# Two large load buffers of a decode-attention kernel begin at multiples of 512 bytes in a partition

## Chip, cores, metric

The kernel runs on one core of one Trainium2 chip. The metric is the device time of one execution in microseconds (us), given as the median of several executions.

## The reference

The kernel computes one decode step of grouped-query attention (2 batches, 32 query heads, 8 key/value heads, 32768 cached positions, head size 128) and a small MLP on the same normalised input, and multiplies the two. Cut to what matters:

```python
def _A_ref(x, k_cache, v_cache, wq, wo):       # x (2,1,512), caches (2,8,32768,128), all bf16
    q = (x @ wq)                               # 32 heads of 128
    scores = einsum("bhqd,bhkd->bhqk", q, k) * Dh ** -0.5
    o = einsum("bhqk,bhkd->bhqd", softmax(scores), v)
    return o @ wo
...
return x + s * silu(mlp(xn))                   # s = _A_ref(xn, ...)
```

The two caches are 268 MB together, and every byte is used once. One query position per batch makes the arithmetic small, so the time to bring the caches in from HBM (the chip's main memory) is what counts.

## The kernel before

Of the sixteen (batch, head) groups, each has one 8 MB load of K and one of V. Every load puts 65536 contiguous bytes into each of the 128 partitions of SBUF, the memory that the compute engines work from. Sixteen DMA engines carry the loads. K lives in `kbuf`, V in `vbuf`; the weights are loaded into parts of the same two buffers that are free at the time. All sizes in `pers` are handed out one after the other in each partition, in the order of the program.

```python
    pers = ctx.enter_context(tc.tile_pool(name="pers", bufs=1))
    ...
    kbuf = pers.tile([128, 3 * SLOT], BF16, name="kbuf")      # SLOT = 16384 elements, 32768 bytes
    vbuf = pers.tile([128, 2 * SLOT], BF16, name="vbuf")
    Ts = [pers.tile([128, RT * NB * 32], I32, name=f"T{i}") for i in range(T_BUFS)]
    # ... some 40 smaller tiles follow

        def load_k(m):
            base = (m % 2) * SLOT
            src = row_view(A_k_cache, *groups[m])             # 128 x 65536 bytes, contiguous
            if m < last:
                d_k[m % 2].after(sp.dma_start(out=kbuf[:, base:base + 2 * SLOT], in_=src), 16)
            # ... the last group goes as two halves
        def load_v(m):
            ...
                sp.dma_start(out=vbuf[:, :], in_=src).then_inc(s_v, 16)
    ...
        for m in range(1, NG):                                # the SP queue issues all these loads
            wait(sp, (p_t, NT * (m - 1) + NR))                # half of K(m-1) has been used
            load_k(m)
            wait(sp, (p_o, m))                                # V(m-1) has been used
            load_v(m)
        # ... then the output projection's weights, wo, in 4096-byte pieces, into kbuf
```

The vector engine (DVE) transposes K in 32x32 blocks, the matrix engine (PE) makes scores, the scalar engine (ACT) takes the exponential, and PE multiplies with V.

The softmax here doesn't subtract the row's maximum and nothing guards it: scores larger than these inputs give would overflow.

## Time and profile before

| | before |
|---|---|
| median of 3 runs (first measurement) | 661.21 us (660.96 to 661.62) |
| span of the profiled run | 659.8 us |
| bytes read | 280.5 MB, mean 425 GB/s |
| PE, DVE, ACT busy | 60%, 51%, 8% |
| load queue's share of sixteen DMA engines | 98.5% |

These are lines of the page of the kernel before. The rows of digits cut the span into 40 equal slices and give the busy share of each in tenths (9 is 90% or more). PEclk is the granted clock of PE in tenths. The last line is a DMA queue: its packets, its megabytes, and the time that its packets took as a share of sixteen engines over the span.

```profile
span 659.8 us, 6521 instructions
...
PE 393.7 (60%) x2684; PEld 165.5 (25%) x2684; DVE 337.0 (51%) x428; ACT 50.3 (8%) x152; POOL 5.7 (1%) x18
...
PE   0538195683829558282865828376481947648765
...
DVE  2347191744809165380926539083562908447650
...
PEclk9999787785978769597885959779596976959795
DMA  8999999999999999999999999999999999999994
GB/s 366 434 443 441 434 445 421 421 445 433 441 442 405 441 434 441 441 445 401 441 433 445 441 413 429 438 441 441 441 401 445 433 445 437 417 429 430 421 421 197
...
q1 hardware_dynamic: 6408, 280.50, 98.5%
```

The DMA row is at 9 from the second slice to the last but one, and the queue's share is 98.5%. PE and DVE have nearly empty slices, and PE's clock falls to half in some, all without any dip of DMA that lasts. The kernel is limited by its loads.

This line of the table of waits has engine, tile and line, what it waited for, the total in us, how often, and the longest. DVE stood idle 150.5 us for K:

```profile
DVE T L449 <- DMA kbuf<-in_A_k_cache_dram: 150.5, 17, 11.4
```

The trace also records each DMA packet with its size and duration. The pages do not print the durations, so they are tabulated here. Here one packet is the bytes of one piece of contiguous destination in one partition (the texts below also call it a descriptor).

| bytes of a packet | packets | shortest | median | mean (ns) |
|---|---|---|---|---|
| 65536 (K and V) | 3840 | 2416 | 2421 | 2422.6 |
| 32768 (wq, last group) | 640 | 1211 | 1216 | 1233.1 |
| 14336 (MLP weights) | 256 | 535 | 535 | 535.1 |
| 4096 (wo) | 1024 | 159 | 161 | 163.3 |

The sum over all of them is 649.8 us for each of sixteen engines. The end of the span, in order of time (start, us, engine, line, operation; in brackets the idle time before it and what ended it):

```profile
...
645.00 3.59 PE L503 MATMUL bank<-vbuf,pt 128*16 128x512 bf16 x32 [5.08 <-DMA vbuf<-in_A_v_cache_dram]
...
652.50 3.58 PE L540 MATMUL bank<-kbuf,oX 128*2 128x128 bf16 x128 [0.47 <-DVE oX L473]
...
656.46 0.29 DVE L549 TENSOR_TENSOR out<-sg,x 98x128 bf16<-98x128 f32 x1
```

PE waits for the second half of the last V load, until 645.00. From there to the end of the arithmetic at 656.75 it is a chain of small steps, 11.75 us long.

### The profile page before, as it was taken

Reading aid. Unit: us, or ns where it says so; the run is one execution under the profiler, and the core shown is the slowest. Engines: PE = TensorE matmul, PEld = TensorE weight load, DVE = VectorE, ACT = ScalarE, POOL = GpSimd, SP = SyncE. Lnnn points to the kernel's source line nnn. Section 1 sums busy time; section 2 is a strip of 40 time slices with the busy share of each in tenths; the row PEclk is TensorE's granted clock in tenths of the full one; section 3 lists DMA queues with packets and bytes.
Section 4 is the critical chain, followed back from the end, with each engine's and each line's share of the span. In section 5 each row is a group of like instructions: output and inputs, shape, how many; then the busy total and the mean of one; then the engine's idle time right before and its main releaser. Section 6 shows DMA issues by size and latency. Waiting matters only on the chain. (4 is left out here: it accounts for less than half of the span.)

```text
span 659.8 us, 6521 instructions
## 1 busy us (share of the span) xinstructions
PE 393.7 (60%) x2684; PEld 165.5 (25%) x2684; DVE 337.0 (51%) x428; ACT 50.3 (8%) x152; POOL 5.7 (1%) x18
## 2 busy tenths in 40 slices
PE   0538195683829558282865828376481947648765
PEld 0513132231313223031322303132131322213223
DVE  2347191744809165380926539083562908447650
ACT  0111001010100101010010101001010010101000
POOL 1200000000000000000000000000000000000000
PEclk9999787785978769597885959779596976959795
DMA  8999999999999999999999999999999999999994
GB/s 366 434 443 441 434 445 421 421 445 433 441 442 405 441 434 441 441 445 401 441 433 445 441 413 429 438 441 441 441 401 445 433 445 437 417 429 430 421 421 197
DMA packets 6443, 280.64 MB, mean 425 GB/s; under 512 B 664, under 2 KB 672, under 8 KB 1696
## 3 DMA queue, kind: packets, MB, share of 16 engines
q1 hardware_dynamic: 6408, 280.50, 98.5%
q8 instruction: 5, 0.08, 0.1%
q14 instruction: 6, 0.05, 0.0%
q10 hardware_dynamic: 24, 0.01, 0.0%
HBM read 280.50 MB, written 0.00 MB: 425 GB/s over the span
## 5 line engine op out<-in xcount | busy, mean ns | idle before, releaser
L486 PE MATMUL bank<-T,z 128*128 128x512 bf16 x1024 | 283.1, 428 | 184.7 <-PEq L45 179.6
L449 DVE STREAM_TRANSPOSE T<-kbuf 128x1024 int32<-128x1024 int32 x256 | 290.6, 1206 | 150.5 <-DMA kbuf<-in_A_k_cache_dram 150.5
L486 PEld LDWEIGHTS bank<-T,z 128*128 128x128 bf16 x1024 | 99.3, 104 | 362.0 <-issue 283.6
L503 PE MATMUL bank<-vbuf,pt 128*16 128x512 bf16 x1024 | 68.2, 426 | 5.1 <-DMA vbuf<-in_A_v_cache_dram 5.1
L466 DVE RECIPROCAL rec<-bank 128x4 f32<-128x4 f32 x16 | 2.9, 182 | 114.2 <-PE bank L513 114.2
L423 ACT ACTIVATE ep<-bank 128x512 bf16<-128x512 f32 x32 | 19.1, 598 | 482.2 <-PE bank L486 482.2
L503 PEld LDWEIGHTS bank<-vbuf,pt 128*16 128x16 bf16 x1024 | 26.4, 98 | 38.8 <-issue 12.6
L457 DVE STREAM_TRANSPOSE pt<-ep 128x512 bf16<-128x512 bf16 x32 | 22.1, 691 | 20.2 <-ACT ep L423 20.2
L496 PE MATMUL bank<-sm,ones_f 128*128 128x4 f32 x64 | 9.4, 252 | 27.6 <-PEq L45 27.6
L513 PE MATMUL bank<-sel_o,ob 128*128 128x4 f32 x128 | 17.2, 258 | 12.5 <-PEq L45 12.5
L513 PEld LDWEIGHTS bank<-sel_o,ob 128*128 128x128 f32 x128 | 16.3, 199 | 20.5 <-issue 20.5
L496 PEld LDWEIGHTS bank<-sm,ones_f 128*128 128x128 f32 x64 | 8.5, 192 | 35.4 <-issue 35.4
L431 ACT COPY ob<-bank 128x512 f32<-128x512 f32 x16 | 9.4, 586 | 87.6 <-PE bank L503 87.6
L411 ACT COPY z<-qr 32x16 bf16<-32x16 bf16 x64 | 12.6, 197 | 0.6
L286 PE MATMUL bank<-ident,xn_bf 2*128 2x2 bf16 x4 | 0.3, 166 | 16.7 <-POOL x L277 16.7
L519 PE MATMUL bank<-on,sel_r 128*128 128x4 bf16 x64 | 3.9, 164 | 9.0 <-PEq L45 9.0
L423 ACT ACTIVATION_READ_ACCUMULATOR ep<-bank 128x1 f32 x32 | 6.3, 198 | 0.2
L470 DVE TENSOR_TENSOR xm<-bank,mask 128x16 f32<-128x16 f32 x16 | 2.8, 175 | 6.8 <-PE bank L519 6.8
L245 DVE CAST xf<-x_bf 128x512 f32<-128x512 bf16 x1 | 0.4, 427 | 11.4 <-DMA x_bf<-in_A_x_dram 11.4
L462 DVE TENSOR_SCALAR sm<-sel_h,rs 128x4 f32<-128x4 f32 x32 | 6.0, 188 | 0.0
L519 PEld LDWEIGHTS bank<-on,sel_r 128*128 128x128 bf16 x64 | 2.9, 97 | 9.9 <-issue 9.9
L322 PE MATMUL bank<-xT,kbuf 128*128 128x2 bf16 x128 | 3.6, 165 | 2.0 <-DVE xT L316 2.0
(64 smaller groups left out, 50.2 us busy)
## 6 DMA issues: line engine op xcount, KB each, us to landing
kbuf<-in_A_k_cache_dram SPq DMA_DIRECT2D x2, 4096.0 KB, 23.7
vbuf<-in_A_v_cache_dram SPq DMA_DIRECT2D x2, 4096.0 KB, 28.9
kbuf<-in_A_wq_dram SPq DMA_DIRECT2D x1, 4096.0 KB, 12.2
vbuf<-in_B_w_dram SPq DMA_DIRECT2D x2, 1792.0 KB, 17.9
kbuf<-in_A_wo_dram SPq DMA_DIRECT2D x1, 2048.0 KB, 38.3
kbuf<-in_A_wo_dram SPq DMA_DIRECT2D x1, 1536.0 KB, 41.5
kbuf<-in_A_wo_dram SPq DMA_DIRECT2D x1, 512.0 KB, 42.1
kbuf<-in_A_k_cache_dram SPq DMA_DIRECT2D x15, 27.7
```

Of the source, the lines that this page charges most:

```text
L322: i = pe.matmul(qT_ps[:, h * B:(h + 1) * B], lhsT=wq3[:, k, h * Dh:(h + 1) * Dh], rhs=xT[:, k, :], start=(k == 0), stop=(k == DK - 1),)
L411: i = act.copy(out=z[32 * j:32 * j + 32, :, :, c:c + rep], in_=qr[32 * j:32 * j + 32, :, :, b, g * rep:(g + 1) * rep],)
L423: act.activation(out=eps_[i][:, :], in_=sc[i][:, :], func=ACT.Exp, scale=inv_sqrt_dh, accum_out=rss[NPART * (m % 2) + i][:, :],)
L431: act.copy(out=ob[:, :], in_=o[:, :]).then_inc(s_ob, 1)
L449: dve.transpose(out=Ts[n % T_BUFS][:, :].rearrange("p (b t k) -> p t b k", b=NB, t=RT), in_=kt[:, r * W:(r + 1) * W].rearrange("p (t b k) ...
L457: dve.transpose(out=pts[h][:, :, :].rearrange("p r (t h) -> p t r h", h=rep), in_=eps_[i][:, :].rearrange("p (t r h) -> p t r h", r=NR, h= ...
L462: dve.tensor_scalar_mul(out=sms[h][:, :], in0=sel_h[:, :], scalar1=rss[NPART * (m % 2) + i][:, 0:1]).then_inc(s_p, 1)
L486: last_mm = pe.matmul(sc[i][:, :], lhsT=z[:, nb, e, zc:zc + 128], rhs=Tb[:, nb, :, e], start=(r == 0 and nb == 0 and e == 0), stop=(r == N ...
L496: pe.matmul(S, lhsT=ones_f[:, :], rhs=sms[h][:, :], start=(h == 0), stop=(h == NPART - 1))
L503: last_mm = pe.matmul(o[32 * j:32 * j + VT * rep, :], lhsT=pts[h][:, r, a * VT * rep:(a + 1) * VT * rep], rhs=vt[:, u * VT:(u + 1) * VT, : ...
L513: last_mm = pe.matmul(oT, lhsT=ob[:, t * Dh:(t + 1) * Dh], rhs=sel_o[:, t, :], start=(t == 0), stop=(t == VT - 1))
L519: last_mm = pe.matmul(xp[:, r, :], lhsT=sel_r[:, r, :, :].rearrange("p j w -> p (j w)"), rhs=on[:, :], start=True, stop=True,)
```

## The change

The intent: begin the destinations of the large loads on a round address, in case the DMA engines write faster there.

```diff
+PAD = 384
 ...
     psum = ctx.enter_context(tc.tile_pool(name="psum", bufs=1, space=bass.MemoryType.PSUM))
 
+    pers.tile([128, PAD // 4], F32, name="pad")
     kbuf = pers.tile([128, 3 * SLOT], BF16, name="kbuf")
     vbuf = pers.tile([128, 2 * SLOT], BF16, name="vbuf")
```

In the built programs, K moves from byte 16512 of a partition to 16896 and V from 114816 to 115200. Before, both are 128 past a multiple of 512 and also 128 past a multiple of 256. Every later tile moves by the same 384 bytes. Instructions, waits, DMAs and packets stay as they were.

## The prediction

> **What bounds the kernel now.** The DMA engines, from end to end. The profile's queue table gives the load queue 98.5% of sixteen engines' span; the 40-slice table shows DMA at 9 in all slices but the first and last, with 401 to 446 GB/s in the slices between. The compute engines have slack: PE 60%, DVE 51%, ACT 8% busy. The table of waits agrees: DVE idles 150.5 us for K loads. The granted clock falls to 0.5 in slices, which costs nothing here, as PE is not the limit.
>
> The trace's records of DMA packets say the same more sharply. The load queue has 3840 packets of 65536 bytes (mean 2423 ns), 640 of 32768 (1233 ns), 1024 of 4096 (163 ns) and 256 of 14336 (535 ns). Their durations sum to 649.8 us per engine, in a span of 659.8. Idle engine time inside the stream is under 1 us. What is left, about 10 us, is the start before the first packet (some 2 us) and the tail after the last (the output projection, 3.6 us of matmuls; two vector operations; the store).
>
> **What the change does.** Built both ways, K moves from byte 16512 of a partition to 16896, V from 114816 to 115200: from 128 past a multiple of 512 (also 128 past a multiple of 256) to a multiple of 512. Everything allocated later moves by 384 bytes too. The order of instructions on every engine, the waits, the number of DMAs, their bytes and packets are the same. So only the duration of one packet can change.
>
> **How much is there to win.** Medians, 65536 bytes against 4096: 2421 - 161 = 2260 ns for 61440 bytes, 27.19 bytes/ns, or 435 GB/s over 16 engines. The Trainium skill, "DMA: Bandwidth & Descriptors", "Where 436 GB/s comes from", puts the ceiling of the ports at 435.2; the trace agrees, so the bytes of a packet already move at that ceiling in spite of the misaligned start. Off that slope there is an intercept of about 10 ns a packet. If alignment costs anything it hides in these 10 ns. The same page, "How a descriptor splits into AXI transactions", says a descriptor that starts off a 256-byte boundary pays a partial first transaction and a leftover, once per descriptor and not once per 256 bytes. An estimate from its 32-byte beats: 4 extra beats on 2048, 0.2%, about 5 ns of 2421; no run yet shows that this holds for the write side in SBUF.
>
> There are 5760 packets, 360 per engine. At 5 ns each that is 1.8 us; all of the 10 ns is 3.6 us (0.5%). All of it would be on the critical path, since DMA is. More likely the intercept is a fixed cost of a packet, and the gain is near zero. Shifts of the other tiles touch DVE, PE and ACT only, whose time is hidden.
>
> **Predicted time:** 660.4 us, 8 in 10 between 657.2 and 662.4. Faster by over 2%: 1%. Within 2%: 98%. Slower by over 2%: 1%.
>
> **What the profile will show.** If right: the mean of 65536-byte packets stays between 2411 and 2425 ns, the load queue's share stays at 98 to 99%, the average at 424 to 427 GB/s, the transpose of K stays at 1202 ns, the waits keep their sizes. If alignment pays its estimated beats: 65536-byte packets about 5 ns shorter, and 4096-byte packets by the same 5 ns rather than in proportion. Wrong, if 65536-byte packets fall below 2405 ns.
>
> **What would make it wrong.** A cost of misalignment that grows with bytes and that the 4096-byte packets share in proportion, so that my slope hides it; that would need a ceiling above 435 GB/s. Or a collision of the shifted buffers with engine reads, which the before trace gives no sign of.

## The result, and the profile after

| | before | after |
|---|---|---|
| median (4 runs each) | 661.09 us (660.90 to 661.62) | 659.13 us (658.75 to 659.45) |
| ratio, 95% interval | | 0.9969 [0.9952, 0.9986] |
| span of the profiled run | 659.8 us | 657.7 us |

A ratio here is the mean time of one kernel's fast runs over that of the other's fast runs of the same rounds, so not quite the ratio of the medians. The change takes off 1.96 us by the medians, 0.3%.

The page after:

```profile
span 657.7 us, 6489 instructions
...
PE 389.4 (59%) x2652; PEld 165.8 (25%) x2684; DVE 336.8 (51%) x428; ACT 50.3 (8%) x152; POOL 5.7 (1%) x18
...
DVE  2447091744809265380926539083562908447650
...
DMA  8999999999999999999999999999999999999995
GB/s 361 438 448 442 439 438 403 446 438 442 438 411 438 439 438 442 423 426 438 438 442 426 423 442 434 447 430 411 446 438 442 438 407 442 438 442 415 425 422 225
...
q1 hardware_dynamic: 6408, 280.50, 98.7%
```

Little moves in these lines. The load queue still fills its sixteen engines (98.7%), and the mean rate rises from 425 to 427 GB/s. The wait of DVE for K is 5 us shorter:

```profile
DVE T L451 <- DMA kbuf<-in_A_k_cache_dram: 145.3, 17, 10.4
```

The end of the span:

```profile
...
642.89 3.59 PE L505 MATMUL bank<-vbuf,pt 128*16 128x512 bf16 x32 [4.88 <-DMA vbuf<-in_A_v_cache_dram]
...
650.39 3.58 PE L542 MATMUL bank<-kbuf,oX 128*2 128x128 bf16 x128 [0.47 <-DVE oX L475]
...
654.36 0.29 DVE L551 TENSOR_TENSOR out<-sg,x 98x128 bf16<-98x128 f32 x1
```

The second half of the last V landed 2.11 us earlier (642.89 against 645.00), and the chain behind it is as long as before (11.76 us). So the whole gain was made in the stream of loads.

The packets show where in the stream. In the kernel before, the 65536-byte packets had durations of 2418, 2419, 2422 and 2426 ns in the main, with 31% at exactly 2418. After, 98% stand at exactly 2418, and the 4096-byte packets at exactly 159, where the median before was 161. The shortest times are the same on both sides to 2 ns (2416 and 2418 at 65536 bytes, 159 at 4096); what went is an extra of 0 to about 13 ns a packet.

| bytes of a packet | mean before | mean after | difference (ns) |
|---|---|---|---|
| 65536 | 2422.6 | 2419.1 | 3.5 |
| 32768 | 1233.1 | 1230.1 | 3.0 |
| 14336 | 535.1 | 535.0 | 0.1 |
| 4096 | 163.3 | 159.5 | 3.8 |

A better measure is the pitch: the time from one packet to the next on an engine. The packets of one engine overlap by a few ns (after the change, durations of 2418 against a pitch of 2414.8), and a duration does not say how much. I take it from the landings of the loads K8 and K14, at the DMA engine that is done first: 96 packets an engine lie between them (six loads of K and six of V, eight packets each). Before it is 2419.1 ns, after 2414.8: 4.3 ns less.

### The profile page after: what moved, and what is told of

Read it like the earlier page. It is cut to its first block, busy times and chain, and to the rows that moved or that the text cites. A ratio compares the mean times of both kernels' runs of the same rounds, so it can differ in the third digit from the quotient of the medians.

```text
span 657.7 us, 6489 instructions
## 1 busy us (share of the span) xinstructions
PE 389.4 (59%) x2652; PEld 165.8 (25%) x2684; DVE 336.8 (51%) x428; ACT 50.3 (8%) x152; POOL 5.7 (1%) x18
## 3 DMA queue, kind: packets, MB, share of 16 engines
q1 hardware_dynamic: 6408, 280.50, 98.7%
## 5 line engine op out<-in xcount | busy, mean ns | idle before, releaser
L488 PE MATMUL bank<-T,z 128*128 128x512 bf16 x992 | 275.4, 424 | 187.1 <-PEq L46 180.5
L505 PE MATMUL bank<-vbuf,pt 128*16 128x512 bf16 x1024 | 71.7, 443 | 4.9 <-DMA vbuf<-in_A_v_cache_dram 4.9
```

The source lines that it names most:

```text
L488: last_mm = pe.matmul(sc[i][:, :], lhsT=z[:, nb, e, zc:zc + 128], rhs=Tb[:, nb, :, e], start=(r == 0 and nb == 0 and e == 0), stop=(r == N ...
L505: last_mm = pe.matmul(o[32 * j:32 * j + VT * rep, :], lhsT=pts[h][:, r, a * VT * rep:(a + 1) * VT * rep], rhs=vt[:, u * VT:(u + 1) * VT, : ...
```

## Experiments

Theory A: the time of a DMA packet depends on where it begins in SBUF, once a packet, and the gain is that alone. Theory B: the same, but only multiples of 512 help. Theory C: the shift of all the other tiles did it, by way of the engines that read and write them.

### K and V alone, and everything else alone

`kv_only` (5 rounds) moves K and V and puts the later tiles 512 bytes on, so that they stand to multiples of 512 as before:

```diff
+    pers.tile([128, 384 // 4], F32, name="pad")
     kbuf = pers.tile([128, 3 * SLOT], BF16, name="kbuf")
     vbuf = pers.tile([128, 2 * SLOT], BF16, name="vbuf")
+    pers.tile([128, 128 // 4], F32, name="pad2")
```

> K and V begin at multiples of 512 bytes, all later tiles stay at 128 past one, as before. Theory A (where a DMA packet begins in SBUF sets its time): the whole gain of the change, ratio 0.997, 64 KB packets nearly all at 2418 ns, 4 KB packets nearly all at 159 ns. Theory C (the other tiles' shift did it, by way of the engines' reads and writes): ratio 1.000, 64 KB packets spread over 2418 to 2426 ns as before.

`rest_only` (5 rounds) leaves K and V and moves the rest:

```diff
     vbuf = pers.tile([128, 2 * SLOT], BF16, name="vbuf")
+    pers.tile([128, 384 // 4], F32, name="pad")
     Ts = [pers.tile([128, RT * NB * 32], I32, name=f"T{i}") for i in range(T_BUFS)]
```

> K and V stay at 128 past a multiple of 512, all later tiles move to multiples of 512. Theory A: ratio 1.000, 64 KB packets spread over 2418 to 2426 ns, mean near 2422.5. Theory C: ratio 0.997, packets at 2418 ns.

### Other starts: 256 and 64

`off256` and `off64` (5 rounds each) are the change with another pad, 128 and 448 bytes:

```diff
+    pers.tile([128, 128 // 4], F32, name="pad")       # off64: 448 // 4
     kbuf = pers.tile([128, 3 * SLOT], BF16, name="kbuf")
```

The page that the next text means is "DMA: Bandwidth & Descriptors", section "How a descriptor splits into AXI transactions".

> K, V and all later tiles at 256 past a multiple of 512. Theory A with a step of 256 bytes (the Trainium skill's page on DMA splits a descriptor at 256-byte boundaries): as good as the change, ratio 0.997, 64 KB packets at 2418 ns. Theory B (512 bytes is what counts): ratio 1.000, packets spread as before.

> K, V and all later tiles at 64 past a multiple of 512. Theory A, cost in beats of 32 bytes below the start (2 where before has 4): half of the cost stays, ratio 0.9985, mean of 64 KB packets near 2420. If any start off a 256-byte boundary costs the same: ratio 1.000, mean near 2422.5.

The four ran on one chip. All gave correct results. Medians, with the kernel before at 661.01 us (9 runs); the pitch is taken as above:

| | K, V begin past 512 at | T begins past 512 at | median us | ratio, interval | mean of 65536-byte packets | pitch (ns) |
|---|---|---|---|---|---|---|
| before (first profile) | 128 | 128 | 661.01 | | 2422.6 | 2419.1 |
| rest_only | 128 | 0 | 661.65 | 1.0007 [0.9994, 1.0021] | 2422.7 | 2419.2 |
| off64 | 64 | 64 | 661.61 | 1.0005 [0.9991, 1.0018] | 2422.7 | 2418.9 |
| kv_only | 0 | 128 | 659.21 | 0.9974 [0.9961, 0.9988] | 2419.8 | 2414.9 |
| off256 | 256 | 256 | 659.09 | 0.9972 [0.9958, 0.9985] | 2419.1 | 2414.9 |
| after (first comparison) | 0 | 0 | 659.13 | 0.9969 [0.9952, 0.9986] | 2419.1 | 2414.8 |

Theory C falls: moving the rest gives nothing, and moving K and V alone gives all of it. Theory B falls: 256 does as well as 512. What counts, of the starts tried, is a multiple of 256. `off64` also corrects theory A in one point. I had written down two possibilities for it: half of the cost, by beats of 32 bytes below the start, or all of it. It was all of it (2418.9 against 2419.1 and, aligned, 2414.8). A start 64 past a boundary costs a packet what 128 past it costs.

### The loads with no work beside them

The extra might still need the compute engines: they use SBUF while the DMA engines write it. The trace of before speaks against it. Of the 65536-byte packets after the first 50 us that stayed under 2440 ns, those with DVE busy under 5% of the time had 3.3 ns over 2418, and those with DVE busy over 95% had 3.5. `dma_mis` and `dma_al` (3 rounds each) test it. They hold the loads of before and of after and nothing else; the output is zeros. Each load waits for the last load of its own buffer to land, so that one is always in flight:

```diff
-            wait(sp, (p_t, NT * (m - 1) + NR))
+            wait(sp, (d_k[(m - 1) % 2], 16 * ((m - 1) // 2 + 1)))
             load_k(m)
-            wait(sp, (p_o, m))
+            sp.wait_ge(s_v, 16 * m)
             load_v(m)
 ... # all PE, ACT, POOL and DVE work taken out, but for the zeros that are stored
```

> All loads of before with nothing else (no matrix, vector or scalar work; the output is zeros, wrong on purpose); buffers at 128 past a multiple of 512. If the DMA engines alone make the spread: 64 KB packets at 2418 to 2426 ns, mean near 2421.6, some 2 us longer than dma_al. If the spread comes from engines that use SBUF at the same time: all packets at 2418 ns and the same time as dma_al.

> The same with buffers at multiples of 512: 64 KB packets at 2418 ns under both theories; about 8 us below the change's time, since the tail of compute is gone. DMA engines alone: ratio to dma_mis 0.997; engines' use of SBUF: 1.000.

Measured: 656.27 us (656.20 to 656.32) and 654.96 us (654.66 to 655.09), 1.31 us apart (ratio 0.998), where some 2 us (0.997) were expected if the DMA engines alone make the extra, and none if not. Both outputs were wrong. In `dma_mis` the packets spread just as in before (2418 to 2426 ns, mean 2421.5; 4096-byte packets 163.4). In `dma_al` 92% stood at 2418 and all of wo's at 159. The profiled spans were 654.4 and 653.3 us.

With no compute at all, the misaligned start costs the same: the pitch is 2419.2 ns against 2414.8. So the DMA engines alone make the extra. The Trainium skill, "SBUF — State Buffer", section "Who interferes with whom", says that DMA never contends with a compute engine; both the trace and this pair agree. One blemish: the profiled run of `dma_al` had a stretch from about 127 to 225 us of its span in which 110 packets took over 2450 ns (3 in all of `dma_mis`). Its cause isn't known, and it lifts the mean of that run to 2420.3. The pitch was taken behind it. It also cost time: from K0 to K8 the first engine took 2419.8 ns a packet and not 2414.8, 0.64 us over 128 packets.

The full kernel gained 0.65 us more than this pair (1.96 less 1.31). Part of that may be the blemish: 360 packets at 4.48 ns (the difference of the two pitches) are 1.61 us, and the fastest run of `dma_al` is 1.61 below the median of `dma_mis`. Whether the runs without a profile had such a stretch isn't known. The next but one experiment goes after the rest.

### Sixteen times as many packets

If the cost comes once a packet, smaller packets must multiply it. The first attempt, `c4k_mis` and `c4k_al` (3 rounds each), kept the whole kernel and its correct result. It loads every second stretch of 4096 bytes by one DMA and the rest by another:

```diff
+        def in_chunks(dst, src, sem):
+            d4 = dst.rearrange("p (c h w) -> p c h w", h=2, w=2048)
+            s4 = src.rearrange("p (c h w) -> p c h w", h=2, w=2048)
+            for h in range(2):
+                sp.dma_start(out=d4[:, :, h, :], in_=s4[:, :, h, :]).then_inc(sem, 16)
 ... # load_k and load_v of all groups but the last; the waits for them count to 32
```

> Before, but each K and V load but the last group's goes as two DMAs that take every second stretch of 4096 bytes, so 4096-byte packets in place of 65536; buffers at 128 past a multiple of 512. Base: some 159.5 ns per 4096 bytes against 151.3 of a 64 KB packet's share, so about 5% slower than before. If a misaligned start costs some 3.9 ns per packet whatever its size: 4 KB packets near 163.4 ns mean, about 15 us slower than c4k_al. If it costs per byte: 159.7 ns, about 2 us slower than c4k_al.

> The same 4096-byte packets with K and V at multiples of 512. Per packet: time over that of c4k_mis about 0.978, packets at 159 to 160 ns. Per byte: about 0.997.

Both were correct. They took 721.60 us (714.38 to 723.70) and 720.35 us (719.18 to 722.39); against before, 1.0886 [1.0820, 1.0952] and 1.0904 [1.0882, 1.0926]. The intervals overlap: this is inconclusive, and neither expectation was met. Both were also slower than the expectation's base, some 5% over before (about 694 us), by 26 to 28 us. The pages:

```profile
span 719.8 us, 6551 instructions
...
GB/s 367 381 372 364 404 372 404 407 384 397 393 398 407 375 409 394 411 397 396 409 372 409 394 411 400 396 410 368 410 380 410 391 381 406 392 405 421 435 409 155
```

```profile
span 717.4 us, 6551 instructions
...
GB/s 366 383 373 356 404 359 402 401 403 420 385 397 414 372 422 362 421 404 386 423 356 418 377 417 387 410 420 372 422 369 421 412 382 421 364 422 412 431 420 162
```

In both streams single slices fall to some 360 GB/s (364 and 356 at the lowest, between the first slice and the last). In the two kernels of the first comparison none there is below 401. The packets say the same: one in a hundred took over 396 ns in the misaligned kernel and over 415 in the aligned one, where the median is 159. Work on K and V beside the loads is not needed for it: from 20 to 42 us of the span, before the first transposition of K at 45.7 us, already 8% of the small packets took over 200 ns in each. The two DMAs read from HBM with gaps of 4096 bytes, and I suppose that this slowed both, far more than a few ns a packet; no run has changed it alone. It was a poor experiment for the question.

The second attempt takes both faults out. `p4k_mis` and `p4k_al` (3 rounds each) build on the loads alone. They read a contiguous 32768 bytes of each partition's row and write it in pieces of 4096 bytes to every second place, so that only the write side is cut:

```diff
+        def pieces(dst, src, sem):
+            d4 = dst.rearrange("p (c h w) -> p c h w", h=2, w=2048)
+            s4 = src.rearrange("p (h c w) -> p h c w", h=2, w=2048)
+            for h in range(2):
+                sp.dma_start(out=d4[:, :, h, :], in_=s4[:, h, :, :]).then_inc(sem, 16)
 ... # used for K and V of all groups but the last; waits count to 32
```

> Loads alone as in dma_mis (zeros, wrong on purpose), but in 4096-byte packets that read one contiguous 32 KB stretch per partition and write every second 4096 bytes of the buffer, at 128 past a multiple of 512. If the misaligned start costs some 3.9 ns per packet: mean of 4 KB packets near 163 ns and about 15 us longer than p4k_al. If the cost is bound to the stream and not to the packet: about 1 to 4 us longer.

> The same at multiples of 512: 4 KB packets at 159 ns, some 690 us. Per packet: time over that of p4k_mis near 0.978; bound to the stream: 0.995 to 0.999.

They took 690.53 us (690.44 to 690.60) and 672.34 us (672.29 to 672.54): 18.2 us apart, or 2.6% (672.34 / 690.53 = 0.974). Outputs were zeros again. The rates of the two pages:

```profile
span 688.8 us, 136 instructions
...
GB/s 365 411 409 410 410 409 410 409 410 410 409 410 410 410 410 409 410 410 409 410 410 410 409 409 410 410 409 410 409 410 409 409 410 410 409 410 430 426 426 305
```

```profile
span 670.8 us, 136 instructions
...
GB/s 360 422 422 421 422 422 422 422 422 422 422 422 422 422 421 422 421 421 422 422 422 422 422 422 422 422 421 421 422 422 422 422 422 422 422 421 443 428 424 311
```

In slice after slice there are 409 or 410 GB/s misaligned and 421 or 422 aligned. Every one of the 62464 small packets of `p4k_al` took exactly 159 ns; those of `p4k_mis` took 159 to 172, mean 163.9. An engine has 3960 packets here, 3904 of them of 4096 bytes. 18.19 us over 3960 is 4.6 ns a packet, and so is the pitch, K8 to K14 (160.0 against 155.4). At 65536 bytes the pitch gave 4.3 to 4.5 (full kernels, loads alone). So the cost is one of about 4.5 ns a packet at both sizes, and not one per byte: a cost per byte would have left the 1.3 to 2 us of the large packets. The MLP weights, whose durations showed no difference, agree. From the landing of wq to that of the second MLP load an engine has 16 packets of 14336 bytes. Their pitch, as the mean of the sixteen engines, is 535.1 to 535.9 ns in the six misaligned kernels so far (`c4k_mis` among them) and 530.7 to 531.2 in the six aligned: again some 4.5 ns.

### Instruction fetches

The profiled spans of before and after differ in two ways at the landing of the last half of V. The DMA engine that is done first is done 1.18 us earlier, counted from the first packet. And the last engine trails the first by 3.23 us, not 4.16. The first fits: 296 packets at 4.3 ns are 1.27 us. The second, 0.93 us, needs another reason, since in the loads alone the last engine trails by 0.3 to 0.7 us throughout. It is no chance of one run: at that landing the last engine trails by 4.51 us in `rest_only` and 4.40 in `off64`, and by 3.44 in `kv_only` and 3.32 in `off256`. So it goes with the start of K and V too.

In the full kernel this lag grows in steps, near 233, 425 and 605 us of the span. At the same times there are records of instruction fetch, of 8192 bytes each. The 65536-byte packet of load that met the fetch near 233 us took 3080 ns in before, `rest_only` and `off64`, and 2948 to 2955 in the change, `kv_only` and `off256`; near 425 us it was 3080 or 3081, and 2948. So I supposed that each fetch costs its engine 0.13 us more when the load is misaligned.

`fetch_mis` and `fetch_al` (5 rounds each) add 2400 small vector instructions to the loads alone, which makes for many fetches:

```diff
+        for i in range(2400):
+            k = V(dve.memset(ln2[:, 0:128], 0.0))
+            wait(dve, k)
         wait(dve, k_x)
         k = V(dve.memset(out4[:, :], 0.0))
```

> dma_mis with 2400 small vector instructions beside it, so some 19 or more instruction fetches of 8 KB share one DMA engine with the loads. Theory: in before, a 64 KB packet that meets a fetch takes about 3080 ns, in the change 2948, and all fetches fall on the engine that ends last. Then each fetch here costs about 0.66 us on that engine, and 0.13 us more than in fetch_al: some 2.5 us on top of the 1.3 us between dma_mis and dma_al, 3 to 4 us in all. If fetches are not part of the gain: 1.3 us between the two.

> The same with buffers at multiples of 512: packets that meet a fetch near 2948 ns; 3 to 4 us (ratio 0.995) below fetch_mis if fetches are part of the gain, 1.3 us (0.998) if not.

They took 674.83 us (674.64 to 675.53) and 672.80 us (672.24 to 672.98), 2.03 us apart. The expectation was 3 to 4 us, so it was missed; it lies nearer to the 1.31 of the pair without fetches. Their pages have DVE idle in the last three slices, so the loads set the end and not the added work:

```profile
...
DVE  6666666666666666666666666666666666665000
...
q14 instruction: 19, 0.16, 0.1%
```

```profile
...
DVE  6666666666666666666666666666666666666000
...
q14 instruction: 19, 0.16, 0.1%
```

A packet that met a fetch took about 3080 ns misaligned and about 3053 aligned: 0.03 us apart, not 0.13. The lag of the last engine was the same in the end (16.55 us both). Both runs also had packets over 2600 ns near 560 to 603 us that met no fetch, 25 in `fetch_mis` and 8 in `fetch_al`, so that their difference is a rough measure. So the size that I gave this effect does not hold in general. Why the full kernel's aligned loads got off with 2948 is open, and so is how the start of K and V makes the 0.9 us of lag.

The pair shows something else. Between the landings of K0 and K14, 542 us apart, there are 17 fetches of 8192 bytes, and in that time the lag of the last engine grows from 1.4 to 18.0 us in `fetch_mis`, about 1.0 us a fetch. A DMA engine's whole stream is delayed, though the fetch itself took 0.3 us and the packet that met it 0.66 us more than 2418 ns, and the load is only done when the slowest of the sixteen engines is. Against `dma_mis`, that is 18.6 us for instructions that do nothing.

## Why the prediction was right

- **The bound.** Right. DMA was full before and after (98.5 and 98.7% of sixteen engines), and all of the gain was made in the stream of loads.
- **The ceiling.** Right. I read 27.19 bytes/ns from two packet sizes and concluded that the bytes already move at the ports' rate, so that only a cost per packet could be won. The Trainium skill ("DMA: Bandwidth & Descriptors", section "Where 436 GB/s comes from") gives 435.2 GB/s; after the change the pitch of 2414.8 ns is 434 GB/s (16 x 65536 / 2414.8). That the ports are what sets it is read from this agreement; no run tests it. No packet of 65536 bytes came near the 2405 ns that I had named as the sign of being wrong.
- **Once a descriptor, at 256 bytes.** Right. The estimate from the same page's section "How a descriptor splits into AXI transactions" was 4 beats of 32 bytes, about 5 ns a packet, the same at 4096 and at 65536 bytes. Measured: 4.3 to 4.6 ns at both, with the step at 256 and not at 512. The count of beats is not confirmed, though: by it, a start at 64 should cost 2 beats, half of what 128 costs, and it cost as much. So the runs show a cost per packet that depends on the start, and not what makes it.
- **The weight I gave it.** This was the weak step: "More likely the intercept is a fixed cost of a packet, and the gain is near zero." Part of the intercept is fixed indeed (159 ns for 4096 bytes is left, at any start), but the alignment's part was real. My own estimate of 1.8 us was near to the measured 1.96, and I marked it down to 0.8 (660.4 us). The range held, but it held a gain of nothing as well. "The waits keep their sizes" belongs to the same doubt: DVE's wait for K fell by 5.2 us.
- **What lies on the critical path.** "All of it", 360 packets an engine, was too many. The last stretch hangs on the second half of V, behind 296 packets; the 64 of wo land under other work. 296 x 4.3 is 1.27 us, of which the first engine shows 1.18. The rest of the gain, 0.93 us in the profiled pair, came from a smaller lag of the slowest engine, which the prediction didn't have. The experiments show that it goes with the start of K and V, and not why. That 1.8 came so near to 1.96 is in part luck: too many packets on the path stood in for a lag that I had not seen.
- **No collision with engine reads.** Right: `rest_only` is unchanged, and the loads alone have the same spread.

Two things stay open. One is small: the durations of the first loads (the 14336-byte packets, and the 65536-byte packets of the first 40 us, 2418.3 ns on average) show next to no extra although misaligned. The cost is there, as the pitch of the 14336-byte packets shows; a duration only doesn't always show it. The other is nearly half of the gain (0.93 of the 2.11 us of the profiled pair): why the slowest engine lags less when K and V are aligned.

## What to carry to other kernels

Where a kernel waits for loads, begin each DMA's destination in SBUF at a multiple of 256 bytes: a misaligned start (64 or 128 past one) cost about 4.5 ns a packet here, which is 0.2% at 64 KB and 2.6% at 4 KB a packet. Before you hope for more, fit bytes against duration for two packet sizes: the slope says whether the bytes are at the ceiling already, and the intercept times the number of packets on the critical path bounds what a cost per packet can give (here a smaller lag of the slowest engine came on top). To see an effect of 0.3% clearly, find what it is counted in and multiply that by sixteen, with everything else taken away.

## What the Trainium skill lacked or had wrong

- "DMA: Bandwidth & Descriptors", section "How a descriptor splits into AXI transactions", describes starts off a 256-byte boundary by what a transaction reads, and does not speak of the write into SBUF. Here the start in SBUF alone was moved, and it cost 4.3 to 4.6 ns a packet; starts at 0 and 256 past a multiple of 512 were alike (pitch 2414.8 and 2414.9 ns).
- By that section's beats, taken over to the write side, a start at 64 costs half of one at 128. It cost the same (pitch 2418.9 and 2419.1 ns).
- "SBUF — State Buffer", section "Operand start alignment", says of its own runs that they timed nothing. For DMA writes the number above is such a time.
- "Runtime: NRT & Kernel Launch", section "Instruction fetch mechanics", calls the cost of a fetch mostly hidden. In a kernel bound by DMA it was not: each fetch of 8192 bytes held back one of the sixteen DMA engines by about 1.0 us, and 2400 idle instructions made the loads 18.6 us longer. The section gives blocks of 16 KiB; the records here have packets of 8192 bytes in one queue (q14) and of 16384 in another (q8).
- "DMA: Bandwidth & Descriptors" has its measured rates of plain copies for contiguous reads and for row pitches of 512 KiB and more. Two DMAs that each read every second 4096 bytes ran at some 356 to 423 GB/s, slice by slice, for most of the stream, and one packet in a hundred took over 396 ns instead of 159 (with compute beside it, though it began before the work on K and V did; pieces cut on the write side alone, with none, did not show this).
